# Order of roundings and low parts, pool places, subtractions and stores in a gated stage with stacked half blocks

## The chip, the cores and the metric

The kernel runs on one core of a Trainium2 chip. The metric is the device time of one execution in microseconds; the time shown for a kernel is the median of several executions. One further execution was taken with the hardware profiler, and all rows come from it. The engines are TensorE (PE; its weight loads are listed as PEld), VectorE (DVE), ScalarE (ACT), GpSimd (POOL) and SyncE (SP). SP and POOL issue nearly all DMAs; POOL does hardly anything else. Each engine executes its instructions in order.

## The reference, cut to what matters

All data are float32; S = 2048 tokens, D = 640, F = 1728.

```python
xn = _layernorm(x)
a = jnp.einsum("bsd,ed->bse", xn, dft_hid_re)
b = jnp.einsum("bsd,ed->bse", xn, dft_hid_im)
A = jnp.einsum("ts,bse->bte", dft_seq_re, a) - jnp.einsum("ts,bse->bte", dft_seq_im, b)
gate = jnp.einsum("bsd,df->bsf", xn, W_gate)
up = jnp.einsum("bsd,df->bsf", xn, W_up)
gate = gate * (gate > 0).astype(gate.dtype)
B = jnp.einsum("bsf,fd->bsd", gate * up, W_down)
return x + A + B
```

## The kernel before, in words

Every matrix product is done in split precision: an operand is rounded to a high part (a copy by ACT, the helper `copy`, L128, or the first line of `split`, L131), and the rest is its low part (a subtraction by DVE, L132 in `split`). A product is then three matmuls (`mm3`, L137 to L139: high x high, high x low, low x high), each 128x128 weights by 128x512 moving columns. Products are arranged in Strassen-Winograd fashion: seven block products with sums S1 to S4 of one operand and T1 to T4 of the other, in place of eight.

The kernel has three stages.

The first stage (`ph0`, `ph1`) normalises x and multiplies it by the sequence DFT matrices, chunk by chunk (four chunks of 512 columns). A chunk is 20 blocks, five kinds (T1, T2, B22, T3, T4) with four groups each. The function `drive` walks over the blocks of all chunks: it issues a block's loads, prepares it (subtraction L712, split L131 and L132) two positions ahead, and runs its matmuls two positions later. Beside that, `token_sets` builds the token operand of the gated stage (steps 0 to 5 for each half q of the tokens): load raw x and row statistics, `make` (subtract and scale, L394/L395 for steps 0 and 1, L417/L418 for the others), `more` (T sums, L424), `halve` (split into two parts), and a `keep` that stores them to DRAM from POOL (L401, L436, L449). `cross_sets` stacks the two parts of a half block over the 128 partitions: four loads on POOL (L464), four subtractions on DVE (L471), six stores on POOL (L475, L476). These pieces are put into the first stage by `hooks`: `at(c, name, g, f)` calls f in the preparation of that block. The hook's place is a place in the text of the program. In the first stage the order on each engine is made by a planner that works with estimated costs and readiness; only instructions that are pinned (`keep_in_program_order`, `pin`, `issue_after`) keep to the program's order. The subtractions L471 and the loads L464 are not pinned.

The gated stage (`ph2`) is a loop of 26 units, 13 column blocks of 128 for each of the two token halves, the second half of the tokens first. Here the order on PE, DVE, ACT and POOL is the written one (`manual_schedule`); SP's is still the planner's. One unit, `gate_up(n)`, has 53 matmuls. In PE's order, with the PSUM banks b1, b4, c, d: A11B11 into b1; S1T1 into b4; S2T2 onto b1; A12B21 onto c, with one short product; S3T3 onto b1; S4B22 onto b4, with one short product each onto b4 and d; A22T4 onto b1, with one short product. Each long product is six matmuls of `mm3` and one matmul with the stacked half blocks (L967); the short ones are L970. ACT copies b1 to c after the first product, b4 to d after the second, b1 to u2 after the third and b1 to u3 after the fifth, and takes the relu of c (L1003) after the fourth. PE may only write onto b1 again when the copy before has been made.

Between these, the weights of the next unit are prepared (`Weights`): SP loads the raw tile z (two units ahead); ACT rounds the half block of the fifth row (`fifth_high`, 64x512) and DVE takes its low part (`fifth_low`, L915); DVE makes the four sums (`sums`, L921 to L924); ACT rounds the sums in two parts (`high_sums(0)`, `high_sums(1)`, 128x768 each), and the own blocks and w5 (`high_own`, 128x1152 and 128x256); DVE takes the low parts of the sums (`low_sums`, 128x1024) and of the own blocks (`low_own`, 128x768), both L937. DVE also makes oa (L1017) and, in the next unit, the three `finals` (L954 to L956), after which POOL stores the result (L957, hd). Further work is put into slots of a unit by lists: `issues` (after the finals), `urgent`, `loads` (before S3T3), `besides` (after u3), `after` (after oa). It is token steps for the other half (units 1 to 9), the cross step (unit 10), loading and splitting the next token sets (`next_set`, units 11, 12 and 24), and from unit 13 on one pair of down-projection weights in each (`pair_weights`: five SP loads L1118, four DVE operations L1123 to L1126, a rounding, a low part L1132, a POOL store L1139).

`gate_up_rest` does the 64 last columns of gate and up, before the first unit for one token half and after the last for the other: relu (rg, L1062), product (hh, L1063), and a store of hh from POOL (hr, L1066). Behind the first of its two products in the second call stands `lead_split`, which prepares the first product of the last stage.

The last stage projects both results with the hidden DFT matrices and W_down (tiles rw or raws for the data, wr for raw weights, cb and wt for their splits) and stores the output.

SBUF tiles come from pools. A pool opened after another was closed takes its bytes, and a tile on bytes that an earlier tile held waits for the users of that tile. In `ph2` the left-hand pools are opened one behind the other in the order of the list; z and zs hold the weights and their sums, hob the results, cx the stacked blocks XT3, XT4 and XB22, fifth the tile w5, and sets the token work and later T sets. `late_place(i)` gives pieces of one large tile, r1, that holds other data in the first stage.

Of the kernel before, what the change touches and what calls it, by code (L numbers as in the profile page):

```python
# [7 lines left out]
F32 = mybir.dt.float32  # L8
# [4 lines left out]
P = 128  # L13
# [50 lines left out]
def fnet_reglu_kernel(  # L64
# [303 lines left out]
    def token_sets(q, step, place=None, unit=None):  # L368
# [15 lines left out]
        if step < 2:  # L384
# [56 lines left out]
            split(h.bitcast(F32R), src.bitcast(F32R), src)  # L441

        if unit:
            unit(load, made[0][0] if step > 1 else [lambda: (make(), halve("a"))], keep_whole)
            return

        def keep(name, place, view):
# [402 lines left out]
        at(c, "B22", 2 * i + 1, *([halve["mr"]] if i else halve.values()))  # L850
    load, subs, keep = cross_sets(1, work_pair)
    at(NCHUNK - 1, "T1", 0, load)
    at(NCHUNK - 1, "T1", 3, *subs[:2])
    at(NCHUNK - 1, "T2", 0, *subs[2:], lambda: defer(1, keep))

    def phase(c, names):

# [29 lines left out]


    ph2 = ExitStack()
    for n, b, side in (("prep", 2, "left"), ("tmp", 1, "left"), ("wr", 1, "left"), ("hob", 2, "left"), ("z", 2, "left"),  # L890
                       ("zs", 1, "left"), ("cx", 1, "left"), ("fifth", 2, "left"), ("sets", 1, "left"), ("gw1", 1, "right")):
        open_pools[n] = ph2.enter_context(tc.tile_pool(name=n, bufs=b, side=side, reuse_waits="tile"))
    pool = open_pools.__getitem__
    get_gw = (get_gw0, lambda: pool("gw1").tile([P, NGW], F32R, name="gw"))
# [48 lines left out]
        def low_own(self):  # L943
            self.low(self.z[:, P3 : 4 * P3], HA, 3, LOWS + 4 * 2 * P)

    issues, urgent, besides, after, loads = ({n: [] for n in range(-1, NU + 2)} for _ in range(5))
    weights, held = {}, {}
    tmp = lambda name, n=CH: pool("tmp").tile([P, n], F32, name=name)
    c0, c1 = slice(0, CH), slice(CH, W2)
# [9 lines left out]
    def gate_up(n):  # L959
        q = 1 - n // NF  # L960
        w, ahead = weights[n].w, weights.get(n + 1)

        def product(ps, a, b, x, first=False, last=False):
            for j in range(2):
                h, l = (w[:, o : o + P] for o in (a * P3 + j * P, LOWS + a * 2 * P + j * P))
                mm3(ps, (h, l), set_half(q, b, j), first and j == 0, False, not first)
            nc.tensor.matmul(ps, w[:, a * P3 + 2 * P : (a + 1) * P3], crossing[q, x], start=False, stop=last, skip_group_check=not first)  # L967
# [12 lines left out]
        if n > 0:  # L980
            finals(n - 1)
        for f in issues[n]:
            f()
        for f in urgent[n]:
            f()
        copy(c, b1)
        if ahead:
            ahead.fifth_low()
            ahead.sums()
        product(b4, S1, T1, XT1, True, True)  # L990
        copy(d, b4)
        if n == NF - 1:
            load_cross(0, "a")
        product(b1, S2, T2, XT2, last=True)
        copy(u2, b1)
        if ahead:
            ahead.high_sums(0)
        product(c, A12, B21, XB21)
        fifth_product(c, A4, 0)
        if ahead:  # L1000
            ahead.high_sums(1)
            ahead.low_sums()
        nc.scalar.activation(ob[:, c0], c, AF.Relu)  # L1003
        if n == NF - 1:
            load_cross(0, "b")
        if ahead:
            ahead.high_own()
            ahead.low_own()
        for f in loads[n]:
            f()  # L1010
        product(b1, S3, T3, XT3, last=True)
        copy(u3, b1)
        for f in besides[n]:
            f()
        product(b4, S4, B22, XB22)
# [31 lines left out]

    def gate_up_rest(q, n):
        w = rest["w"]
        rg, hh = (late_place(i) for i in (3, 4)) if n else (place(i) for i in (0, 1))  # L1050
        a, b = slice(0, REST), slice(REST, 2 * REST)
        for c in range(2):
            ps = bank()
            part = [set_half(q, (B11, B12)[c], 0), set_half(q, (B11, B12)[c], 1),
                    set_half(q, (B21, B22)[c], 0), set_half(q, (B21, B22)[c], 1), set_half(q, X4, c)]
            for k in range(KD):
                mm3(ps, (w[:, 0, k * P : (k + 1) * P], w[:, 1, k * P : (k + 1) * P]),
                    part[k], k == 0, k == KD - 1)
# [4 lines left out]
            tt(hh[a, cs], ps[a], rg[a, cs], op=OP.mult)  # L1063
            if n and c == 0:
                lead_split()
        issues[0 if n is None else NU + 1].append(lambda: nc.gpsimd.dma_start(hrest[q], hh[a]))  # L1066
# [10 lines left out]

    def token_step(step, n):

        def unit(load, make, keep):  # L1080
            issues[n - 1].append(load)
            for i, m in enumerate(make):
                besides[n + i].append(m)
            issues[n + len(make)].append(keep)

        token_sets(0, step, spot, unit)

# [19 lines left out]
    def pair_weights(k, n):  # L1107
# [26 lines left out]
        loads[n - 1].append(load)  # L1134
        besides[n].append(prepare)
        after[n].append(lows_of)
        def keep():
            z = t["z"]
            nc.gpsimd.dma_start(wparts[:, k], z[:, RA:Y21])  # L1139
            if k == NPAIR - 1:  # L1140
                h, l = (z[:REST, o + Y22 : o + Y22 + 2 * P] for o in (HIGH, LOW))
                for rows, v, o in ((0, 0, h), (0, 1, l), (REST, 0, l), (REST, 1, h)):
                    nc.gpsimd.dma_start(wend[rows : rows + REST, v * 2 * P : (v + 1) * 2 * P], o)

        issues[n + 1].append(keep)

    def pair(k0, n):

# [23 lines left out]
        lead["b"], lead["w"] = b, w  # L1172

    loads[NU - 2].append(lead_load)
    for step, n in enumerate((1, 1, 2, 4, 6, 8)):
        token_step(step, n)

    def cross_step(n):
        load, subs, keep = cross_sets(0, lambda: pool("prep").tile([P, END], F32, name="pw")[:, : 2 * W2])
        issues[n - 1].append(load)  # L1180
        besides[n] += subs
        issues[n + 1].append(keep)

    cross_step(10)
    next_set(X4, 9)
    for i, n in ((T2, 11), (T1, 11), (T3, 11)):
        next_set(i, n)
    next_set(B11, NF - 1, lambda: place(3), low=besides)
    next_set(B21, NF - 1, lambda: place(4), low=besides)
    next_set(T4, NF - 1)  # L1190
    next_set(B22, NF - 1, lambda: place(5), high=after, low=urgent, later=1)
    next_set(B12, 24, lambda: late_place(2))
# [312 lines left out]
```

## Time and profile before

| what | value |
|---|---|
| runs, median (lowest to highest) | 1043.58 us (1043.14 to 1045.24), 3 runs |
| the profiled execution | 1044.09 us |
| its span, first to last instruction | 1041.9 us |
| mean granted TensorE clock | 0.993 |
| gated stage, units 0 to 25 | about 414 to 734 us of the span |
| DMA moved | 266.43 MB, mean 256 GB/s |

How to read the rows: a wait row names the engine and the tile it works on, who released it, the total in us, the number of times and the longest. A timeline row has start, duration, engine, line, operation, out<-in, shape, count, and in brackets the idle time of that engine before it with what ended it. A row of the chain of waits has start, duration and what the time was. A stretch row has the stretch, its length, the busy time of PE, PEld, DVE, ACT and POOL with the number of instructions, the granted clock, the DMA share and GB/s. A row on DMA issues has out<-in, queue, count, KB of each and the median us from issue to landing. Times in rows count from the start of the span. PE's busy time overlaps itself a little: a matmul row lasts 0.39 us while the next one starts 0.23 us after it.

### The profile page before, as it was taken

The numbers are of one execution on the slowest core, as the hardware profiler recorded it, in microseconds if no ns is written. First come the engines' busy times: TensorE is split into PE (matmuls) and PEld (weight loads), VectorE is DVE, ScalarE is ACT, GpSimd is POOL, SyncE is SP. The second block draws the span as 40 slices with busy tenths as digits, with TensorE's granted clock in tenths as the row PEclk, the third lists the DMA queues.
The fourth block names the chain that finished last, engine by engine and source line by source line (L and its number), as shares of the span: only waits on it lengthen the run. The fifth ranks groups of instructions, "written<-read, shape, count | busy, mean of one in ns | idle before, by whom it ended". The sixth has DMA issues, their size and how long they took to land.

```text
span 1041.9 us, 12615 instructions
## 1 busy us (share of the span) xinstructions
PE 1019.1 (98%) x4498; PEld 840.7 (81%) x4498; DVE 810.7 (78%) x1085; ACT 487.2 (47%) x659; POOL 135.2 (13%) x215
## 2 busy tenths in 40 slices
PE   9999999999979999999999999999899999999998
PEld 8888888888867888778888788878688888888887
DVE  7967977999949777587778888877586896767983
ACT  5644453343432334455556665555344434443432
POOL 3521011022131001122221000101000001000000
PEclk9999999999999999999999999999899999999999
DMA  8897735859868976766659777785899477897624
GB/s 319 318 300 279 249 125 175 318 203 320 330 220 291 381 296 242 233 232 215 211 204 344 284 279 252 230 299 216 289 357 324 130 255 220 280 323 233 219 91 142
DMA packets 94142, 266.43 MB, mean 256 GB/s; under 512 B 11776, under 2 KB 32832, under 8 KB 91264
## 3 DMA queue, kind: packets, MB, share of 16 engines
q1 hardware_dynamic: 73584, 185.12, 52.1%
q0 software_dynamic: 20064, 79.97, 21.0%
q8 instruction: 35, 0.57, 0.2%
q10 hardware_dynamic: 432, 0.56, 0.1%
q14 instruction: 27, 0.22, 0.1%
HBM read 198.74 MB, written 65.81 MB: 254 GB/s over the span
## 4 chain that ended last, share of the span: by engine, by line
PE 63%; issue 24%; DMA 5%; DVE 3%; POOL 3%; ACT 1%; SPq 0%; POOLq 0%; ACTq 0%; DVEq 0%
PE ps L137 19%; PE ps L138 19%; PE ps L139 19%; PE ps L546 3%; PE ps L967 2%; DMA cx<-cross 1%; DMA wparts<-pw 1%; PE ps L970 1%; PE ps L576 1%; DMA pw<-in_wd 1%; PE ps L1350 1%; POOL set L449 1%; DMA sets_b<-rows 1%; DMA r<-in_xt 1%; ACT gw L128 0%
## 5 line engine op out<-in xcount | busy, mean ns | idle before, releaser
L131 ACT ACTIVATE cb<-rw 128x1024 fp32r<-128x1024 f32 x83 | 81.7, 987 | 138.9 <-PE ps L139 97.8
L131 ACT ACTIVATE cb<-raw 128x1024 fp32r<-128x1024 f32 x71 | 75.3, 1060 | 124.5 <-PE ps L139 116.3
L132 DVE TENSOR_TENSOR cb<-rw,cb 128x1024 fp32r<-128x1024 f32 x83 | 93.9, 1132 | 49.3 <-ACT cb L131 48.9
L132 DVE TENSOR_TENSOR cb<-raw,cb 128x1024 fp32r<-128x1024 f32 x71 | 86.8, 1222 | 37.6 <-ACT cb L131 37.2
L137 PE MATMUL ps<-cb,wt 128*128 128x512 f32 x270 | 105.9, 394 | 4.4 <-ACT wt L131 4.4
L138 PE MATMUL ps<-cb,wt 128*128 128x512 f32 x270 | 105.6, 393 | 0.0
L139 PE MATMUL ps<-cb,wt 128*128 128x512 f32 x270 | 105.4, 392 | 0.0
L138 PE MATMUL ps<-cb,xs_late 128*128 128x512 f32 x232 | 90.3, 389 | 0.0
L137 PE MATMUL ps<-cb,xs_late 128*128 128x512 f32 x232 | 90.3, 389 | 0.0
L139 PE MATMUL ps<-cb,xs_late 128*128 128x512 f32 x232 | 90.3, 389 | 0.0
L137 PE MATMUL ps<-cb,xs_early 128*128 128x512 f32 x226 | 87.9, 389 | 0.0
L138 PE MATMUL ps<-cb,xs_early 128*128 128x512 f32 x226 | 87.9, 389 | 0.0
L139 PE MATMUL ps<-cb,xs_early 128*128 128x512 f32 x226 | 87.9, 389 | 0.0
L937 DVE TENSOR_TENSOR gw<-zs,gw 128x1024 fp32r<-128x1024 f32 x26 | 31.9, 1226 | 46.4 <-ACT gw L128 46.4
L137 PEld LDWEIGHTS ps<-cb,wt 128*128 128x128 f32 x270 | 51.2, 190 | 15.5 <-ACT wt L131 4.8
L128 ACT ACTIVATE gw<-z 64x512 fp32r<-64x512 f32 (+1 forms) x52 | 46.4, 893 | 32.4 <-PE ps L967 25.9
L138 PE MATMUL ps<-xs_early,gw 128*128 128x512 f32 x156 | 60.8, 390 | 0.0
L137 PE MATMUL ps<-xs_early,gw 128*128 128x512 f32 x156 | 60.7, 389 | 0.0
L139 PE MATMUL ps<-xs_early,gw 128*128 128x512 f32 x156 | 60.7, 389 | 0.0
L138 PEld LDWEIGHTS ps<-cb,wt 128*128 128x128 f32 x270 | 51.4, 190 | 10.8
L139 PEld LDWEIGHTS ps<-cb,wt 128*128 128x128 f32 x270 | 51.1, 189 | 10.6
L131 ACT ACTIVATE cb<-tk 128x1024 fp32r<-128x1024 f32 x32 | 33.9, 1060 | 46.6 <-PE ps L139 28.9
(219 smaller groups left out, 2413.2 us busy)
## 6 DMA issues: line engine op xcount, KB each, us to landing
raw<-in_dft SPq DMA_DIRECT2D x94, 512.0 KB, 6.4
z<-in_wgu SPq DMA_DIRECT2D x26, 896.0 KB, 5.6
wd<-wparts SPq DMA_DIRECT2D x30, 512.0 KB, 5.0
wparts<-pw POOLq DMA_DIRECT2D x12, 1152.0 KB, 5.8
hd<-ob POOLq DMA_DIRECT2D x26, 512.0 KB, 3.4
rw<-hd SPq DMA_DIRECT2D x24, 512.0 KB, 7.5
tk<-in_dft SPq DMA_DIRECT2D x16, 512.0 KB, 6.8
set<-r POOLq DMA_DIRECT2D x16, 512.0 KB, 4.3
```

The lines of the kernel that those rows point to most:

```text
L128: return nc.scalar.activation(o, i, AF.Copy)
L131: nc.scalar.activation(hi, src, AF.Copy)
L132: return nc.vector.tensor_tensor(lo, src, hi.bitcast(F32), op=OP.subtract)
L137: nc.tensor.matmul(ps, wh, mh, start=first, stop=False, skip_group_check=more)
L138: nc.tensor.matmul(ps, wh, ml, start=False, stop=False, skip_group_check=more)
L139: nc.tensor.matmul(ps, wl, mh, start=False, stop=last, skip_group_check=more)
L449: nc.gpsimd.dma_start(place(v), view(part))
L546: start["pe"] = pin([nc.tensor.matmul(E[0, key], xn_part(n * SG + j, d)[v == 1], b[:, int(v == 2), j], start=False, stop=n % NH == NH - 1 ...
L576: pin([nc.tensor.matmul(E[c, key], xn_part(j, d)[v == 1], b[c][0][:, int(v == 2), j], start=j == 0 and v == 0, stop=False)])
L937: tt(self.w[:, o : o + n * 2 * P].rearrange("p (k n) -> p k n", k=n), main(src), main(self.w[:, at : at + n * P3]).bitcast(F32), op=OP.sub ...
L967: nc.tensor.matmul(ps, w[:, a * P3 + 2 * P : (a + 1) * P3], crossing[q, x], start=False, stop=last, skip_group_check=not first)
L970: nc.tensor.matmul(ps, weights[n].w5[:, a : a + P], set_half(q, X4, c)[0], start=False, stop=True, skip_group_check=True)
```

## The change

Five things are done together.

1. The order inside a unit of the gated stage. On ACT, `high_own` goes from behind the relu to behind u2; `high_sums(0)` from behind u2 to behind the relu; `high_sums(1)` from in front of the relu to behind u3. On DVE, `low_own` and `low_sums` go behind what is in `besides`, and the order of the two is exchanged. Two slots are new: `between` (after d) and `middle` (after the relu).
2. Token steps 0 and 1 of the other half: step 0 is made in unit 0, step 1 in unit 1 (both in unit 1 before), and their halves go into `between` of the next unit; the keep of step 1 goes out one unit later. The loads of both stay in front of the first unit. The high part of the next set B11 goes from `besides` to `middle`, and the low part of B21 from `besides` to `after`, in unit 12.
3. The list of pools of `ph2`: cx and fifth are opened ahead of z, zs and hob. In `gate_up_rest`, rg and hh of the second call are tiles of the pool z in place of `late_place(3)` and `late_place(4)`.
4. The hooks of the four subtractions of `cross_sets` in chunk 3: from T1 group 3 and T2 group 0 to T2 group 3 and B22 group 2; its keep is deferred from there.
5. The keeps of `pair_weights` and of `cross_step` go from `issues` of unit n + 1 to `after` of unit n.

```diff
@@ cross_sets' hooks, first stage
-    at(NCHUNK - 1, "T1", 3, *subs[:2])
-    at(NCHUNK - 1, "T2", 0, *subs[2:], lambda: defer(1, keep))
+    at(NCHUNK - 1, "T2", 3, *subs[:2])
+    at(NCHUNK - 1, "B22", 2, *subs[2:], lambda: defer(1, keep))
@@ pools of the gated stage
-    for n, b, side in (("prep", 2, "left"), ("tmp", 1, "left"), ("wr", 1, "left"), ("hob", 2, "left"), ("z", 2, "left"),
-                       ("zs", 1, "left"), ("cx", 1, "left"), ("fifth", 2, "left"), ("sets", 1, "left"), ("gw1", 1, "right")):
+    for n, b, side in (("prep", 2, "left"), ("tmp", 1, "left"), ("wr", 1, "left"), ("cx", 1, "left"), ("fifth", 2, "left"),
+                       ("z", 2, "left"), ("zs", 1, "left"), ("hob", 2, "left"), ("sets", 1, "left"), ("gw1", 1, "right")):
@@ gate_up
         copy(d, b4)
+        for f in between[n]:
+            f()
...
         copy(u2, b1)
         if ahead:
-            ahead.high_sums(0)
+            ahead.high_own()
         product(c, A12, B21, XB21)
         fifth_product(c, A4, 0)
-        if ahead:
-            ahead.high_sums(1)
-            ahead.low_sums()
         nc.scalar.activation(ob[:, c0], c, AF.Relu)
...
+        for f in middle[n]:
+            f()
         if ahead:
-            ahead.high_own()
-            ahead.low_own()
+            ahead.high_sums(0)
         for f in loads[n]:
             f()
         product(b1, S3, T3, XT3, last=True)
         copy(u3, b1)
+        if ahead:
+            ahead.high_sums(1)
         for f in besides[n]:
             f()
+        if ahead:
+            ahead.low_own()
+            ahead.low_sums()
         product(b4, S4, B22, XB22)
@@ gate_up_rest
-        rg, hh = (late_place(i) for i in (3, 4)) if n else (place(i) for i in (0, 1))
+        rg, hh = (pool("z").tile([P, NRAW], F32, name="z")[:, :W2] for _ in range(2)) if n else (place(i) for i in (0, 1))
@@ token_step
-        def unit(load, make, keep):
-            issues[n - 1].append(load)
+        def unit(load, make, halve, keep):
+            issues[max(n - 1, 0)].append(load)
             for i, m in enumerate(make):
                 besides[n + i].append(m)
-            issues[n + len(make)].append(keep)
+            if halve:
+                between[n + 1].append(halve)
+            issues[n + len(make) + bool(halve)].append(keep)
@@ pair_weights, and the same line in cross_step
-        issues[n + 1].append(keep)
+        after[n].append(keep)
@@ steps and next sets
-    for step, n in enumerate((1, 1, 2, 4, 6, 8)):
+    for step, n in enumerate((0, 1, 2, 4, 6, 8)):
...
-    next_set(B11, NF - 1, lambda: place(3), low=besides)
-    next_set(B21, NF - 1, lambda: place(4), low=besides)
+    next_set(B11, NF - 1, lambda: place(3), high=middle, low=besides)
+    next_set(B21, NF - 1, lambda: place(4))
```

More of the change, by code (lines that the diff above doesn't have):

```diff
@@ L443, in token_sets @@
         if unit:
-            unit(load, made[0][0] if step > 1 else [lambda: (make(), halve("a"))], keep_whole)
+            unit(load, made[0][0], (lambda: halve("a")) if step < 2 else None, keep_whole)
             return
@@ L944, in low_own @@
             self.low(self.z[:, P3 : 4 * P3], HA, 3, LOWS + 4 * 2 * P)
-    issues, urgent, besides, after, loads = ({n: [] for n in range(-1, NU + 2)} for _ in range(5))
+    issues, urgent, between, middle, besides, after, loads = ({n: [] for n in range(-1, NU + 2)} for _ in range(7))
     weights, held = {}, {}
@@ L1181, in cross_step @@
         besides[n] += subs
-        issues[n + 1].append(keep)
+        after[n].append(keep)
     cross_step(10)
```

## The prediction

> **What bounds the kernel now.** I read the page's busy shares first, then the waits of TensorE (PE), then stretches cut at the starts of the gated stage's units, and last the rows around each gap.
>
> ```profile
> PE 1019.1 (98%) x4498; PEld 840.7 (81%) x4498; DVE 810.7 (78%) x1085; ACT 487.2 (47%) x659; POOL 135.2 (13%) x215
> ...
> PE ps L138 <- DVE cb L132: 8.2, 1, 8.2
> PE ps L137 <- ACT wt L131: 4.4, 1, 4.4
> PE ps L137 <- ACT u L128: 3.0, 3, 1.7
> ```
>
> PE is the bound: busy 98% of the span. The matmuls stay as they are, so the change can win PE's waits and what follows them, no more. By stretches (the stretch and its length; busy time of PE, PEld, DVE, ACT, POOL; granted clock; DMA share and GB/s) the gated stage reads:
>
> ```profile
> 414.07:428.09 14.02, 12.31 (x55) 9.87 (x53) 8.72 (x13) 7.20 (x13) 0.55 (x1) 1.00 0.84 298
> 440.10:453.85 13.75, 12.63 (x55) 9.79 (x53) 11.62 (x18) 6.88 (x12) 2.74 (x5) 1.00 0.49 177
> 465.86:477.87 12.01, 12.01 (x54) 9.95 (x53) 8.81 (x14) 6.30 (x11) 2.10 (x3) 1.00 0.65 240
> 561.97:574.20 12.23, 12.23 (x54) 9.87 (x53) 10.09 (x13) 8.79 (x14) 0.54 (x1) 1.00 1.01 379
> 574.20:588.39 14.19, 12.50 (x55) 9.79 (x53) 12.80 (x20) 8.74 (x13) 0.53 (x1) 1.00 0.84 312
> 684.49:698.04 13.55, 12.63 (x54) 9.79 (x53) 11.65 (x21) 7.69 (x12) 1.07 (x2) 1.00 0.81 285
> ```
>
> An undisturbed unit takes 12.01 us for 53 matmuls. Five of 26 are longer: unit 0 by 2.01, unit 2 by 1.74, unit 12 by 0.22, unit 13 by 2.18, unit 22 by 1.54. The waits of 8.2 and 4.4 us lie outside, one in the third chunk of the first stage (it ends at 314.7), one where the gated stage ends (749.5); each is followed by slow matmuls:
>
> ```profile
> 314.70:317.90 3.20, 3.13 (x8) 2.52 (x9) 3.20 (x5) 0.00 (x0) 0.00 (x0) 0.52 0.75 260
> 749.50:754.70 5.20, 5.17 (x12) 4.11 (x13) 5.20 (x7) 4.27 (x6) 0.00 (x0) 0.50 0.59 176
> 754.70:760.00 5.30, 5.30 (x25) 4.34 (x25) 3.41 (x4) 2.84 (x4) 0.00 (x0) 1.00 0.94 315
> ```
>
> At full clock 25 matmuls start in 5.30 us (about 0.22 each), at clock 0.50 only 12 in 5.20. So the wait of 4.4 us has a tail of (23 less 12) x 0.22 = 2.5, together 6.9 us. The wait of 8.2 has one of (14 less 8) x 0.22, about 1.4: 9.6 us.
>
> The Trainium skill (TensorE: Matmul & The Clock Gate, Part 1) lets the clock drop after an idle window of about 3.4 us and rise again after about 3.4 us of work. The trace has clock 0.5 behind both long waits and behind none of the short ones, as that says; but the tail here lasts 5.2 us. By the page's 3.4 us the second wait would be worth some 0.8 us less than I take.
>
> **The change, part by part.**
>
> *Places of the pools.* cx and fifth together take as many bytes as hob (a 768 KB tile and two of 128 KB against two of 512 KB), and z and zs lie between: cx and fifth swap places with hob, z and zs stay. At the end, cx lay on the first stage's sums; now it lies on its raw tiles.
>
> ```profile
> 400.45 1.23 DVE L132 TENSOR_TENSOR cb<-raw,cb 128x1024 fp32r<-128x1024 f32 x1 [0.68 <-ACT cb L131]
> ...
> 408.65 2.97 DMA pq<-sa
> ...
> 411.75 12.07 DMA cx<-cross
> ...
> 423.87 0.50 PE ps L967
> ```
>
> The load of cx waited until the last sums were stored (408.65 + 2.97), took 12.07, and PE waited for it in unit 0. The last read of a raw tile ends at 401.7; from there even 12.07 us end at 413.8, before unit 0 starts. Unit 0's 2.01 us go. What is late next: hob, now on the sums, is first written in unit 0, which starts at 414.07, after the sums' store landed at 411.6. That cover is 2.5 us; without it the gate's copy waits, whose reader is a unit away.
>
> *rg and hh of the rest.* They move from the r1 block to two z tiles.
>
> ```profile
> 741.58 1.05 ACT L131 ACTIVATE cb<-rw 128x1024 fp32r<-128x1024 f32 x1
> 748.63 0.84 ACT L131 ACTIVATE wt<-wr 128x768 fp32r<-128x768 f32 x1 [6.00 <-issue]
> ...
> 742.70 0.53 POOL L1066 DMA_DIRECT2D hr<-r  x1 [6.76 <-DVE r L1063]
> ...
> DMA to landing us min/median/max: 5.9/5.9/5.9
> ...
> 734.73 0.38 SPq L1295 DMA_DIRECT2D wr<-in_hid  x1
> ...
> wr<-in_hid SPq DMA_DIRECT2D x1, 384.0 KB, 5.9
> rw<-hd SPq DMA_DIRECT2D x3, 512.0 KB, 9.5
> ```
>
> The first wt tile of the last stage lies on the r1 block, so its copy waits for the store of hh: 742.70 + 5.9 = 748.6, and ACT starts at 748.63. The weight itself landed at 734.73 + 5.9 = 740.6. With hh elsewhere ACT copies at 742.6 (0.84), DVE's low part is there near 745, and PE, whose wait began at 745.1 (749.5 less 4.4), goes on. The z tiles are free (unit 25 is the last), and what lies on them in the last stage is its B21 input, due two products later. Bounds: all 6.9 us, or none if the next wait takes its place (rival 2); the rows show nothing else that holds the copy, so I take 6.9.
>
> *Order within a unit.* Shown in unit 13, the worst:
>
> ```profile
> 582.33 1.72 ACT L128 ACTIVATE gw<-zs 128x768 fp32r<-128x768 f32 x2 [2.34 <-DVE zs L922]
> 583.96 0.58 ACT L1003 ACTIVATE ob<-ps 128x512 f32<-128x512 f32 x1
> 584.44 1.15 ACT L128 ACTIVATE gw<-z 128x1152 fp32r<-128x1152 f32 x1
> 585.49 0.40 ACT L128 ACTIVATE w<-z 128x256 fp32r<-128x256 f32 x1
> 585.80 0.58 ACT L128 ACTIVATE u<-ps 128x512 f32<-128x512 f32 x1
> ...
> 580.37 0.69 DVE L915 TENSOR_TENSOR z<-z,gw 64x512 f32<-64x512 f32 x1
> 581.68 0.56 DVE L922 TENSOR_TENSOR zs<-zs,z 128x384 f32<-128x384 f32 x1
> 584.09 1.23 DVE L937 TENSOR_TENSOR gw<-zs,gw 128x1024 fp32r<-128x1024 f32 x1 [0.91 <-ACT gw L128]
> 585.62 0.96 DVE L937 TENSOR_TENSOR gw<-z,gw 128x768 fp32r<-128x768 f32 x1 [0.31 <-ACT gw L128]
> 586.50 0.42 DVE L1123 TENSOR_TENSOR pw<-pw 128x256 f32<-128x256 f32 x1
> ```
>
> PE cannot overwrite b1 until u3 is copied (585.80); in ACT's queue that copy stands behind five others, the first of which waits for DVE's sums. After the change ACT takes own + w5 (1.15 + 0.40), which need only L915: 581.1 to 582.7; the gate 0.58 (583.2); one sum rounding 0.85 (584.1); u3 0.58 (584.7). PE wants it after 45 of the unit's matmuls, near 584.5, so I leave 0.3 of 2.18. Unit 12 has one more copy on that path (the high part of B11, now in `middle`, about 1 us): I put it at 0.3. Unit 2 was long because the halves of both token steps sat in unit 1 and pushed DVE and ACT into unit 2 (DVE 11.62 us there). Now one step is made in unit 0 and one in unit 1, and each half falls into ACT's idle time behind d. Its 1.74 go. Units 2, 12 and 13: 4.14 less 0.6, so 3.5.
>
> The other side: both low parts now come last on DVE, behind `besides`. From the unit's start DVE has three finals of about 0.7, L915 0.69 and four sums of 0.56 (5.0 us), a pair's four operations of 0.42 (6.7), then the own low of 0.96 (behind own, about 8). The sums' low waits for the second sum rounding, which follows u3: its product ends after 36 matmuls (8.3), so 8.9 + 0.85, and the low part ends at 11, in unit 13 near 12.7. PE wants them at its 3rd and 10th matmul, 12.5 and 14.0. This is a cover of 1.3 us at worst and 3 as a rule, so I cost it at nothing; with the cover gone it is rival 4.
>
> *The two stores.* Pair stores (and the cross stores) go out behind the low parts, no longer behind the next unit's finals: Pool issues them some 3 us earlier, ahead of hd, which is ready later anyway.
>
> ```profile
> wparts<-pw POOLq DMA_DIRECT2D x12, 1152.0 KB, 5.8
> ...
> 664.25 11.22 DMA wparts<-pw
> ...
> 684.96 0.44 DVE pw L1123
> ```
>
> Unit 22 was long because one store took 11.22 us, twice the median; the load into its tile followed it, and DVE started that pair only at 684.96, when unit 22 (684.49) had begun. 3 us earlier puts it at 682, before the end of its own unit. Bounds 0 and 1.54; I take 1.5.
>
> The Trainium skill (DMA: Bandwidth & Descriptors, Queues, rings and completion order) has each DMA engine take turns between the queues that have work, so an earlier store only takes its time from the loads beside it; by that rule unit 22 keeps its 1.5 us. The trace has stores of half and of twice that length under the same kinds of transfer and settles nothing.
>
> *The subtractions.* Rows of DVE and POOL around the 8.2 us, and one of DVE's later:
>
> ```profile
> 312.89 0.69 DVE L471 TENSOR_TENSOR r<-r 128x512 fp32r<-128x512 f32 x1 [12.50 <-DMA r<-set]
> ...
> 307.84 0.55 POOL L464 DMA_DIRECT2D r<-set  x1
> ...
> 341.13 2.36 DVE L712 TENSOR_TENSOR tk<-tk,raw 128x1024 f32<-128x1024 f32 x2
> ```
>
> DVE stood for 12.50 us at the first subtraction, whose fourth load was issued only at 307.84; the low part that PE needed (cb L132) stood behind it. But the program places that subtraction behind chunk 3's fourth T1 block, whose own subtraction is the second of the two at 341.13. It ran 29 us ahead of its place: the planner takes it as a filler as soon as it believes the loads landed, and nothing pins it. The new place is six blocks further back, unpinned as well. What pulled it forward over ten blocks should pull it over sixteen. Bounds 0 and 9.6; I take 0, since the row shows that the place did not bind.
>
> **Sum.** 2.0 + 6.9 + 3.5 + 1.5 = 13.9 us. The profiled execution took 1044.09 us (its span of 1041.9 and 2.2 around it), 0.5 above the runs' median of 1043.58. So 1030.2 profiled, 1029.7 for the median.
>
> **Rivals.**
> 1. The later place does free DVE, and the wait that ends at 314.7 goes too. For it: in its new place the operands would have landed long before. Against: the 29 us. 1029.7 less 9.6 is 1020.1.
> 2. The boundary keeps its gap: another load takes the place of hh's store, and rw loads took 9.5 us there. Against: what the first product needs landed at 740.6. 1029.7 + 6.9 = 1036.6.
> 3. Units 12, 13 and 22 keep most of their loss, DVE being late in them for its own load (12.80 and 11.65 us busy). 1029.7 + 3 = 1032.7.
> 4. Slower: the low parts come too late for the next unit, since a pair's operations wait for a load and the low parts now stand behind them. It decides once they end over 3 us later than I reckon in most of the 25 units. At 1 us past that in each: 1029.7 + 25 = 1054.7; break-even is 0.56 us. Against it: DVE idles 2 to 3 us in a unit (8.81 to 10.09 of 12.01 busy), and the earlier store brings the loads forward.
>
> **How the numbers follow.** Forecast 0.46, rival 1 0.30, rival 3 0.10, rival 2 0.08, rival 4 0.06. The range runs from rival 1 with 2.6 us of slack to beyond rival 3: 1017.5 to 1034. This kernel's measurement tells about 0.2% (2 us) from no change. All cases but the last are faster by more; 0.03 I keep for losses that cancel: faster 0.92, same 0.03, slower 0.05.
>
> **What would show it.** cx loaded before 414 and unit 0 at 12.0 us; ACT's first wt copy near 742.6 less what was won before, and no clock of 0.5 there; all units at 12.0 but for 0.3 in 12 and 13; the wparts store near 12.5 us into its unit. L471 idle for some 12 us in front of a low part of the third chunk bears out the planner's argument; its absence, with a time near 1020, is rival 1. PE waiting for DVE's gw (L937) at unit starts would prove me wrong.

## The result and the profile after

The changed kernel took 1030.14 us (median of 4 runs, 1029.97 to 1032.61) beside 1043.42 us for the kernel before: a ratio of 0.9875, 95% interval 0.9856 to 0.9893. The forecast was 1029.7 us. The profiled execution took 1029.97 us, its span is 1027.9 us.

The page's busy shares after the change:

```profile
PE 1014.6 (99%) x4498; PEld 840.0 (82%) x4498; DVE 808.8 (79%) x1085; ACT 488.1 (47%) x659; POOL 135.3 (13%) x215
```

and the waits of TensorE (us in total, times, longest):

```profile
PE ps L138 <- DVE cb L132: 9.0, 1, 9.0
PE ps L119 <- PEq L1506: 0.8, 1, 0.8
PE ps L576 <- DVE xs_early L337: 0.2, 1, 0.2
```

Of the profile before, the row of unit 0's wait belongs beside them:

```profile
PE ps L967 <- DMA cx<-cross: 1.7, 1, 1.7
```

One long wait is left: for DVE's low part in the first stage, 9.0 us where it was 8.2. The waits for `wt` (4.4), `u` (3.0) and `cx` (1.7) are gone. Stretches of the profile after (columns as in the prediction): units 0, 2, 12, 13 and 22, and then 6 us on either side of 740 us, where the last stage has begun:

```profile
414.84:426.85 12.01, 12.01 (x54) 9.95 (x53) 8.06 (x12) 7.04 (x12) 0.55 (x1) 1.00 0.79 275
438.87:450.88 12.01, 12.01 (x55) 9.95 (x53) 10.61 (x17) 6.94 (x12) 1.68 (x3) 1.00 0.42 151
559.00:571.01 12.01, 12.01 (x54) 9.95 (x53) 11.01 (x15) 9.29 (x14) 0.53 (x1) 1.00 1.01 392
571.01:583.03 12.02, 12.02 (x55) 9.95 (x54) 11.85 (x19) 8.29 (x14) 0.53 (x1) 1.00 0.80 284
...
679.13:691.15 12.02, 12.02 (x55) 9.95 (x54) 9.72 (x17) 7.16 (x12) 1.07 (x2) 1.00 0.79 287
733.99:740.00 6.01, 6.01 (x28) 5.00 (x27) 5.39 (x8) 5.35 (x8) 1.08 (x2) 1.00 1.05 406
740.00:746.00 6.00, 6.00 (x29) 4.95 (x27) 5.19 (x7) 4.40 (x6) 0.00 (x0) 1.00 1.06 407
```

All five units are at 12.01 or 12.02 us with TensorE busy from end to end, and so are the other 21; the start of the last stage runs at clock 1.00.

TensorE runs the same 4498 matmuls in the same order in all the kernels of this study, so the time between the same two matmuls can be subtracted from one profile to the next. The table gives this for stretches between fixed matmuls (named by what lies there; us against the profile before; minus is shorter). The last column is the end of the last matmul.

| kernel | start, to 30 us | wait in chunk 3 | chunk 4 | unit 0 | unit 2 | units 12, 13 | 14 to 22 | 23 to the rest | boundary | sum |
|---|---|---|---|---|---|---|---|---|---|---|
| the change | -0.10 | +0.93 | -0.06 | -2.01 | -1.73 | -2.39 | -1.53 | 0 | -7.10 | -13.99 |
| a_subs_back | +0.99 | +1.50 | -0.06 | -2.01 | -1.73 | -2.39 | -1.53 | 0 | -7.10 | -12.34 |
| a_pin | +0.04 | -9.88 | +9.27 | -2.01 | -1.73 | -2.39 | -1.53 | 0 | -7.10 | -15.32 |
| a_pin_mid | +0.11 | -9.88 | +8.23 | -2.01 | -1.73 | -2.39 | -1.53 | 0 | -7.10 | -16.31 |
| a_pin_back | +1.13 | -9.88 | -0.06 | -2.01 | -1.73 | -2.39 | -1.53 | 0 | -7.10 | -23.58 |
| a_stores_back | -0.16 | +0.01 | -0.06 | -2.01 | -1.73 | -1.73 | -1.53 | 0 | -7.10 | -14.29 |
| a_lows_late | +0.58 | +0.93 | -0.06 | -2.01 | -1.73 | +6.50 | +1.95 | +1.94 | -7.10 | +1.00 |
| b_rest_z | -0.02 | +0.95 | -0.06 | -0.15 | -0.01 | +0.01 | +0.52 | 0 | -7.10 | -5.86 |
| b_pools | -0.01 | -0.48 | -0.06 | -2.01 | -0.01 | +0.04 | -1.27 | 0 | +0.30 | -3.49 |
| b_order | -0.05 | -0.17 | +0.05 | -1.34 | +0.51 | -0.63 | -1.53 | 0 | -0.23 | -3.39 |
| b_order_sets | +0.49 | +1.41 | -0.06 | -1.08 | +2.10 | -2.39 | -1.53 | 0 | -0.01 | -1.06 |
| b_tokens | -0.04 | +0.20 | -0.06 | -1.10 | -1.73 | 0 | +0.02 | 0 | +0.24 | -2.45 |
| b_stores | +0.90 | +0.53 | -0.06 | -0.87 | -0.01 | 0 | -1.53 | 0 | -0.34 | -1.36 |

A name with `a_` is the changed kernel with something altered, with `b_` the kernel before with one part of the change (b_order_sets has two). The table is read by columns. Where a transfer decides, a stretch that no edit touches still varies from profile to profile: over a range of 1.3 us in unit 0 and at the start, 2.0 in chunk 3, 1.8 in units 14 to 22 and 0.6 at the boundary. In chunk 4 and units 2, 12 and 13 it is the same to 0.1 us.

The runs were taken in several groups, in which the kernel before had medians of 1042.1 to 1043.4 us; a ratio below is to the kernel before in the same group, so times of two groups compare only to about 1 us. Medians and ratios leave out slow runs, of the kernels here one of b_stores (1719.59 us). Of b_pools, b_order, b_order_sets, b_tokens and b_stores the interval reaches 1.0: their times alone show no gain, and what is said of them is read from one profile each.

### The profile page after: what moved, and what is told of

The parts are those of the page before. It is cut to its first block, busy times and chain, and to the rows that moved or that the text cites. A ratio compares the mean times of both kernels' runs of the same rounds, so it can differ in the third digit from the quotient of the medians.

```text
span 1027.9 us, 12621 instructions
## 1 busy us (share of the span) xinstructions
PE 1014.6 (99%) x4498; PEld 840.0 (82%) x4498; DVE 808.8 (79%) x1085; ACT 488.1 (47%) x659; POOL 135.3 (13%) x215
## 4 chain that ended last, share of the span: by engine, by line
PE 93%; issue 4%; POOL 1%; DVE 1%; DMA 1%; ACT 0%; POOLq 0%; DVEq 0%; ACTq 0%
PE ps L138 27%; PE ps L139 27%; PE ps L137 27%; PE ps L967 4%; PE ps L546 3%; PE ps L970 2%; PE ps L576 1%; PE ps L1358 1%; POOL set L449 1%; DMA cross<-r 0%; PE ps L1363 0%; DVE cb L132 0%; DMA r<-in_x 0%; POOL r L464 0%; POOL pq L685 0%
## 5 line engine op out<-in xcount | busy, mean ns | idle before, releaser
L128 ACT ACTIVATE ps<-ps 128x512 f32<-128x512 f32 (+1 forms) x53 | 30.6, 578 | 59.8 <-PE ps L967 55.4
```

Source lines behind the costliest of these rows:

```text
L128: return nc.scalar.activation(o, i, AF.Copy)
```

## The experiments

### The subtractions: their place, and whether it binds

The changed kernel with the old places (a_subs_back):

```diff
-    at(NCHUNK - 1, "T2", 3, *subs[:2])
-    at(NCHUNK - 1, "B22", 2, *subs[2:], lambda: defer(1, keep))
+    at(NCHUNK - 1, "T1", 3, *subs[:2])
+    at(NCHUNK - 1, "T2", 0, *subs[2:], lambda: defer(1, keep))
```

> The changed kernel with only the subtractions of the first stage's cross operands put back to their two old places (behind the fourth T1 block and the first T2 block of the fourth chunk), free as before. Theory: the place does not bind, DVE takes them in the third chunk in both cases; 1030.1 us within 1 us, with the same wait near 315 us. Rival: the later place made the wait longer or shorter by itself (the wait was 8.2 us before and is 9.0 after): a difference of 0.8 us, 1029.3 us, and no more. Second rival: the old place hurts the fourth chunk: over 1032 us.

The changed kernel with the subtractions kept in program order (a_pin):

```diff
-            return lambda: nc.vector.tensor_tensor(o().bitcast(F32R), i0(), i1(), op=OP.subtract)
+            def run():
+                i = nc.vector.tensor_tensor(o().bitcast(F32R), i0(), i1(), op=OP.subtract)
+                return tc.keep_in_program_order(i) if q else i
+            return run
```

> The changed kernel with one difference: the four subtractions of the first stage's cross operands (L471) are kept at their program place, in the fourth chunk, and may no longer run ahead. Theory: the wait of 9.0 us that is left (TensorE behind DVE's low part in the third chunk, at 315.5 us) comes only from these subtractions running ahead of their loads; with its tail at clock 0.50 it costs 9.2 + 0.4 + 1.4 = 11.0 us, so the time is 1030.1 - 11.0 = 1019.1 us (1018.5 to 1020.5), and the subtractions run after 340 us with no idle time of DVE in front of them. Rival A: the load itself (its issue on POOL at 308 us) holds something else up, and a wait of several us turns up in another place: 1024 to 1030 us. Rival B: the pin makes DVE wait in the fourth chunk instead: 1030 us or more.

Both edits together (a_pin_back):

> The changed kernel with the four subtractions at their old places (behind the fourth T1 block and the first T2 block of the fourth chunk) and kept in program order there. Theory: the pin is what counts and the place does nothing, since the loads have landed (at about 313 us) long before the old place (about 341 us): 1019.1 us, as with the pin at the new places. Rival: the old place is too early even when it is kept (the low parts of T1 and T2 blocks are then late by the 0.6 us of each subtraction): up to 4 x 0.6 = 2.4 us more than with the pin at the new places.

Measured (median, and in brackets the ratio to the kernel before with its 95% interval): a_subs_back 1029.99 us (0.9888, 0.9872 to 0.9903), a_pin 1028.33 us (0.9869, 0.9853 to 0.9884), a_pin_back 1019.18 us (0.9781, 0.9763 to 0.9798), the fastest of all. DVE's rows of the changed kernel around the wait (start, length, what; the idle time before it in brackets):

```profile
313.63 0.69 DVE L471 TENSOR_TENSOR r<-r 128x512 fp32r<-128x512 f32 x1 [13.34 <-DMA r<-set]
314.24 1.22 DVE L132 TENSOR_TENSOR cb<-raw,cb 128x1024 fp32r<-128x1024 f32 x1
```

and POOL's:

```profile
308.45 0.55 POOL L464 DMA_DIRECT2D r<-set  x1
```

With the late places the subtraction still stands in chunk 3, as early as before; DVE stood 13.34 us at it until its last load, issued at 308.45, had landed. So the place did not bind, in either direction: in a_subs_back too the four subtractions run from 313.9 us on, and its time is within 0.2 us of the change (its profile is 1.65 us longer, at the start and in chunk 3, where profiles vary anyway). The wait in chunk 3 is decided by where that subtraction floats: with the pin 9.88 us go in every one of the three kernels (8.56 from one matmul to the next less the usual 0.22, and the tail).

But a_pin won only 1.8 us over the change by the medians, 1.3 by the profiles, where the theory had 11. Its longest wait of TensorE:

```profile
PE ps L137 <- ACT cb L131: 6.6, 1, 6.6
```

The longest wait for a DMA in SP's queue from 340 to 400 us (the next is 3.6 us):

```profile
SPq L792 <- DMA cross<-r: 7.2, 1, 7.2
```

And two steps of the chain of waits there, which end in TensorE's wait:

```profile
376.71 14.03 DMA raw<-in_dft
390.76 1.23 DVE raw L715
```

The late place was harmless only because it was ignored. Once it binds, the third store of the results (L479 there) leaves at 366.14 and lands at 374.37. The next loads of the operand sets (L792) go onto the same block and wait for that landing in SP's queue for 7.2 us; then three loads of 1024 KB and one more go out in one go, and the input loads behind them take 14.03 us (landed at 390.74; in a_pin_back they took 8.0 at the median). With the old place, pinned, those three loads were out at 348.5. In size this is rival A, but the cause is neither rival's: it is the late store of the results, not the load of the operands. a_pin_back came to within 0.1 us of its theory's time, but the theory's words that the place does nothing were wrong: with the pin the two places are 9.2 us apart.

The pin, with the last two one block earlier, behind T2 group 3 (five loads stand between the two blocks; the expectation counts two blocks) (a_pin_mid):

```diff
-    at(NCHUNK - 1, "T2", 3, *subs[:2])
-    at(NCHUNK - 1, "B22", 2, *subs[2:], lambda: defer(1, keep))
+    at(NCHUNK - 1, "T2", 3, *subs, lambda: defer(1, keep))
```

> The changed kernel with the subtractions of the first stage's cross operands kept in program order, the last two brought forward by two blocks (all four behind the fourth T2 block of the fourth chunk). With the pin at the change's own places the third store of the results left at 366.1 us and landed at 374.4; SP's queue stood there for 7.2 us, since the next loads go onto the same block, and four input loads behind it came late; TensorE waited 6.6 us. Theory: the wait follows that landing one for one; the third store leaves near 364 us, lands 2 us (368 to 372) earlier or more, and the wait shrinks by as much: 1022 to 1026 us. Rival: the wait has another cause (the 14 us that the input loads took) and stays near 6.6 us: 1028 us.

Measured: 1027.61 us (0.9847, 0.9819 to 0.9876; 2 runs). TensorE's longest wait in a_pin_mid:

```profile
PE ps L137 <- ACT cb L131: 4.9, 1, 4.9
```

The store landed 2.78 us earlier (371.59), the wait shrank by 1.64, the stretch by 1.04. Not one for one: the input loads left 3.08 us earlier and landed only 1.58 us earlier, behind the large loads issued ahead of them, which landed 3.1 to 3.7 us after one another. The theory's 1022 to 1026 us missed. The landing of the store decides when the queue goes on; how long the backlog then takes is the other part, which this run does not split further.

### The parts of the change alone

rg and hh alone (b_rest_z):

```diff
-        rg, hh = (late_place(i) for i in (3, 4)) if n else (place(i) for i in (0, 1))
+        rg, hh = (pool("z").tile([P, NRAW], F32, name="z")[:, :W2] for _ in range(2)) if n else (place(i) for i in (0, 1))
```

> The kernel before with one part of the change: rg and hh of the rest at the gated stage's end lie in two z tiles, not on the r1 block. Theory: ACT's copy of the first weight tile of the last stage no longer waits for the store of hh; the wait of 4.4 us at the boundary and its tail of 2.5 us at clock 0.50 both go: 1043.4 - 6.9 = 1036.5 us, and no stretch of clock 0.50 near 750 us. Rival A (the wait goes, the clock's drop has another cause): 1043.4 - 4.4 = 1039.0 us. Rival B (another wait takes its place, such as the 9.5 us loads of rw): 1041 to 1043.4 us. By the Trainium skill (TensorE: Matmul & The Clock Gate, Part 1), whose 3.4 us of work bring the clock back, the tail would be worth 1.7 us and the time 1037.3 us.

Measured: 1036.94 us (0.9951, 0.9935 to 0.9966). The boundary is 7.10 us shorter, the same as in the whole change; no wait for `wt` is left. Of the prediction's 6.9 this confirms both halves: 4.56 us go at the first matmul behind the wait and about 2.5 in the ones after it, so the tail was not shorter than the sum took it. The other columns moved by +1.2 together (chunk 3 +0.95); the loss of unit 22 turned up in unit 21 here, 2.06 us long.

The pools alone (b_pools):

```diff
-    ... ("wr", 1, "left"), ("hob", 2, "left"), ("z", 2, "left"), ("zs", 1, "left"), ("cx", 1, "left"), ("fifth", 2, "left"), ...
+    ... ("wr", 1, "left"), ("cx", 1, "left"), ("fifth", 2, "left"), ("z", 2, "left"), ("zs", 1, "left"), ("hob", 2, "left"), ...
```

> The kernel before with only the places of the pools changed (cx and fifth swap with hob). Theory: the load of cx starts once the last raw tile is read (near 402 us) and not after the last store of the sums (411.6 us); unit 0 falls from 14.02 to 12.0 us: 1043.4 - 2.0 = 1041.4 us. Rival: hob on the sums' place makes the gate's copy wait for that store instead, and some of the 2.0 us stays.

Measured: 1042.43 us (0.9994, 0.9979 to 1.0009). In the profile unit 0 is 2.01 us shorter and no wait for cx is left; nothing else comes in its place there. In the changed kernel's profile the load leaves at 402.5 and takes 4.5 us:

```profile
L823 SPq DMA_DIRECT2D cx<-cross x1: 326/326/326, 402.5 to 402.5; - x1
...
DMA to landing us min/median/max: 4.5/4.5/4.5
```

The table's column for unit 0 also shows that before's 2.01 was the longest of its kind: the kernels that keep the old places lost 0.7 to 1.9 there (2.01 less 1.34 to 0.15). In four of them (b_order, b_tokens, b_stores, b_order_sets) the same load took 10.7 to 11.2 us; in the profile before 12.07.

The order in the unit alone (b_order; here and below the lines `if ahead:` are left out):

```diff
-            ahead.high_sums(0)
+            ahead.high_own()
         product(c, A12, B21, XB21)
...
-            ahead.high_sums(1)
-            ahead.low_sums()
         nc.scalar.activation(ob[:, c0], c, AF.Relu)
...
-            ahead.high_own()
-            ahead.low_own()
+            ahead.high_sums(0)
...
         copy(u3, b1)
+            ahead.high_sums(1)
         for f in besides[n]:
             f()
+            ahead.low_own()
+            ahead.low_sums()
```

> The kernel before with only the order inside a unit changed: own rounding ahead of the sums' two, the sums' second rounding behind the copy of u3, both low parts last; token steps, the high part of B11 and the stores stay. Theory: unit 13 falls from 14.19 to 12.0 us (the copy of u3 no longer stands behind the sums' roundings), unit 12 keeps 0 to 0.2, unit 2 keeps its 1.7 (its cause is the two token steps' halves), unit 22 keeps its 1.5 (its cause is the late load): about 1043.4 - 2.2 = 1041.2 us. Rival A: the order also cures units 2 and 22, since in every late unit the copy of u3 stood behind the sums: 1043.4 - 5.4 = 1038.0 us. Rival B: the low parts, last now, come too late in the units whose own DVE work is longest (2, 13, 22): one of them grows.

Measured: 1041.54 us (0.9994, 0.9979 to 1.0009), and in the profile, beside a shorter unit 13, a new wait of TensorE:

```profile
PE ps L139 <- DVE gw L937: 3.3, 2, 1.9
```

Unit 12 is at 12.01 and unit 13's old wait is gone, but units 2 and 13 now begin with one: TensorE waited 1.9 us until 441.15 and 1.3 until 574.92 for their low parts, so unit 2 grew to 14.26 and unit 13 only fell to 13.77. That is rival B, and the mechanism of the prediction's fourth rival. DVE's rows before the second wait:

```profile
571.63 2.36 DVE L1106 TENSOR_TENSOR xs_early<-pw,xs_early 128x1024 fp32r<-128x1024 f32 x2 [2.96 <-ACT xs_early L128]
573.91 0.95 DVE L937 TENSOR_TENSOR gw<-z,gw 128x768 fp32r<-128x768 f32 x1
```

The low parts stood behind an input's low part of 2.36 us that waited 2.96 us for its high part. Unit 22 became whole, though the stores' code was not touched: ten of the twelve pair stores now leave 15.5 us after their unit's start; before they left after 15.8 to 18.6.

The same, with the places of two inputs (b_order_sets; `middle` is run behind the gate's function):

```diff
-    next_set(B11, NF - 1, lambda: place(3), low=besides)
-    next_set(B21, NF - 1, lambda: place(4), low=besides)
+    next_set(B11, NF - 1, lambda: place(3), high=middle, low=besides)
+    next_set(B21, NF - 1, lambda: place(4))
```

> The kernel before with the order inside a unit, and the places of two inputs of the last units of the first half (the high part of B11 behind the gate's function, the low part of B21 behind the unit's last sum); token steps, pools, rest and stores stay. With the order alone units 2 and 12 or 13 grew, TensorE waiting for DVE's low parts (gw, L937) by 1.9 and 1.3 us. Theory: these two inputs' parts held up the low parts near 573 us; that wait goes and units 12 and 13 are at 12.0 us together, while unit 2 stays at 14.3, its low parts behind a token step's operations. Rival: the wait near 573 us stays, and it is the token steps or the pair's load that the low parts stand behind.

Measured: 1042.12 us (0.9989, 0.9978 to 1.0001). With the two inputs out of the way units 12 and 13 are 2.39 us shorter together, both at 12.01, as in the change. Unit 2 has its wait of 1.9 us for the low parts again, and 1.6 more by a tail at clock 0.57 (below): theory on both counts, but for the tail.

The token steps alone (b_tokens, shortened; `between` is run behind the copy of d, `halve` splits steps 0 and 1 into their two parts):

```diff
-            issues[n - 1].append(load)
+            issues[max(n - 1, 0)].append(load)
...
+            if halve:
+                between[n + 1].append(halve)
-            issues[n + len(make)].append(keep)
+            issues[n + len(make) + bool(halve)].append(keep)
...
-    for step, n in enumerate((1, 1, 2, 4, 6, 8)):
+    for step, n in enumerate((0, 1, 2, 4, 6, 8)):
```

> The kernel before with only the token steps moved: the first is made in unit 0 and the second in unit 1, and the halves of each fall behind the copy of d in the unit after. Theory: unit 2 falls from 13.75 to 12.0 us, nothing else changes: 1043.4 - 1.7 = 1041.7 us. Rival: the halves (DVE's 1.2 us and ACT's 1.1 us) move the loss into unit 1 or keep it in unit 2, as the sums' roundings still stand before the copy of u3: 1043 to 1044 us.

Measured: 1041.79 us (0.9987, 0.9975 to 1.0). Unit 2 is 1.73 us shorter, no unit beside it grew. So unit 2 is the token steps', and it is the token steps' move that lets the new order stand in unit 2: the order without it makes unit 2 longer (b_order, b_order_sets).

The stores alone (b_stores; the same line in the pairs and in the cross operands):

```diff
-        issues[n + 1].append(keep)
+        after[n].append(keep)
```

> The kernel before with only the two kinds of stores moved (the pair's and the cross operands' store go out behind the low parts, not behind the next unit's finals). Theory: the pair stores are issued some 3 us earlier in a unit, the loads into their tiles follow, and the loss of 1.5 us in unit 22 goes: 1043.4 - 1.5 = 1041.9 us. Rival (by the Trainium skill, DMA: Bandwidth & Descriptors, Queues, rings and completion order, an earlier store only takes turns with the loads beside it): unit 22, or the unit ahead of it, keeps about 1.5 to 2 us: 1043.4 us. A store that still takes over 8 us, with the load behind it landing over 10 us into its unit, would bear the rival out.

Measured: 1042.68 us (0.9994, 0.997 to 1.0018). In the profile unit 22 is whole, all pair stores but two took 4.4 to 5.4 us, and the pairs' loads, all but the last, landed before their unit began. In b_stores and in the changed kernel alike, by the page's DMA issues (KB each, median us to landing):

```profile
wparts<-pw POOLq DMA_DIRECT2D x12, 1152.0 KB, 4.4
hd<-ob POOLq DMA_DIRECT2D x26, 512.0 KB, 3.8
```

An earlier store did not take its time from the loads here: its own median fell from 5.8 to 4.4 us, and that of the loads of z from 5.6 to 4.7 in b_stores; only the stores of hd became longer, from 3.4 to 3.8. The Trainium skill (DMA: Bandwidth & Descriptors, Queues, rings and completion order) has each DMA engine take turns between queues with work; by that, the prediction said, unit 22 would keep its 1.5 us, and the run did not bear that out. Why the stores became shorter no run here shows.

### Two tests of the changed kernel

The stores put back (a_stores_back; the same line in the pairs and in the cross operands):

```diff
-        after[n].append(keep)
+        issues[n + 1].append(keep)
```

> The changed kernel with only the two kinds of stores put back behind the next unit's finals. The prediction's step: unit 22 or one beside it gets its 1.5 us again, 1030.1 + 1.5 = 1031.6 us. Theory after the runs of single parts (the order alone and the stores alone each made unit 22 whole): the order already issues the pair's store earlier (15.5 us after the unit's start, against 15.8 to 18.6), so no unit grows and the time stays at 1030.1 us; the stores' move is then worth nothing beside the order. The pair's store goes out near 15.5 us in its unit and its load lands 2 to 4 us into the next but one, not before its start.

Measured: 1030.58 us (0.9876, 0.9847 to 0.9904; 2 runs). Units 14 to 22 stay whole, unit 13 is 0.66 us longer (12.68). So beside the order the stores are worth 0.7 us at most, not in unit 22: there either of the two edits is enough.

The low parts one step later (a_lows_late):

```diff
-            ahead.low_own()
-            ahead.low_sums()
         product(b4, S4, B22, XB22)
         fifth_product(b4, A4, 1)
         tt(oa, b4, u2, op=OP.add)
         for f in after[n]:
             f()
+            ahead.low_own()
+            ahead.low_sums()
```

> The changed kernel with both low parts of the next unit's weights moved one step further back, behind the sum of oa and the pair's low part. It measures the cover that the prediction gave the low parts (1.3 us at worst, about 3 as a rule; beyond it each us late in 25 units is 25 us). In a unit with a pair: oa ends about 10.9 us into the unit, the pair's low part 11.9, the own low part 12.8, the sums' 14.0; TensorE wants them at 12.5 and 14.0. Theory: 0.3 us late in the 12 units with a pair, none in the others: 1030.1 + 4 = 1034 us (1031 to 1038), and TensorE waits for DVE's gw (L937). Rival A: the cover is larger than reckoned: no change, 1030.1 us. Rival B: lateness runs up from unit to unit, as the finals and the sums behind them come later too: over 1045 us.

Measured: 1043.99 us (1.0007, 0.9982 to 1.0032; the runs from 1040.62 to 1049.49), 13.9 us over the change and outside both the theory and its rivals. Its waits of TensorE:

```profile
PE ps L138 <- DVE cb L132: 7.7, 1, 7.7
PE ps L139 <- DVE gw L937: 5.9, 3, 2.6
```

Units 14 to 24 are 12.40 or 12.41 us each, so the low parts are late by the 0.3 to 0.4 us expected in each. Units 12, 13 and 25, which follow the units where token sets are prepared too (`next_set`), lost 4.5, 4.0 and 1.5 us; those the expectation had left out. One step further back on DVE would have eaten the whole gain of the change.

## Why the prediction was right

Term by term, with the profile's stretches (forecast, measured):

- Pools, 2.0: 2.01. Both halves of the argument showed: the load no longer waits for the sums' store, and unit 0 shows no wait of TensorE. The term was sized from one draw of the transfer, though; the draws of other kernels were 0.7 to 1.9, so that it fits to 0.01 is luck.
- Boundary, 6.9: 7.10. ACT copies the first weight tile at 735.63; the forecast was 742.6 less what was won until then, 6.9, so 735.7. ACT's rows after:

```profile
734.68 1.05 ACT L131 ACTIVATE cb<-rw 128x1024 fp32r<-128x1024 f32 x1
735.63 0.84 ACT L131 ACTIVATE wt<-wr 128x768 fp32r<-128x768 f32 x1
```

- Order, 3.5: 4.12 (1.73 and 2.39). The step that failed is the 0.6 left in units 12 and 13. For unit 13 it let the copy of u3 end at 584.7, 10.5 us into the unit; in the changed kernel it ends after 9.7 us (unit 13 starts at 571.01, unit 14 at 583.03). ACT's rows after:

```profile
577.48 1.17 ACT L128 ACTIVATE gw<-z 128x1152 fp32r<-128x1152 f32 x1 [0.86 <-DVE z L915]
...
580.07 0.59 ACT L128 ACTIVATE u<-ps 128x512 f32<-128x512 f32 x1
```

and DVE's:

```profile
576.76 0.69 DVE L915 TENSOR_TENSOR z<-z,gw 64x512 f32<-64x512 f32 x1
...
581.83 1.22 DVE L937 TENSOR_TENSOR gw<-zs,gw 128x1024 fp32r<-128x1024 f32 x1
...
592.75 1.23 DVE L937 TENSOR_TENSOR gw<-zs,gw 128x1024 fp32r<-128x1024 f32 x1 [1.13 <-ACT gw L128]
```

Two things were taken wrongly: L915 stands 5.75 us into the unit and not at its old 6.17, and the four copies from own to u3 take 2.59 us from start to start where the sum of their rows gave 2.98 (each row's length reaches into the next row): 0.4 us each, together the 0.8. The low part of the sums ends 12.04 us into unit 13 and 10.95 into unit 14: the prediction had 12.7 and 11. Its cost of nothing was right, and its cover as thin as said (a_lows_late). What the prediction did not say is that this cover exists only with the token steps and the two inputs moved as well (b_order).
- Stores, 1.5 in unit 22: 1.53, but not theirs alone. The order gives the same. The kernels with neither lost 0.3 (b_pools), 1.5 (before, b_tokens) and 2.1 us (b_rest_z, in unit 21), so this size was a draw too. Right sum, wrong share. The prediction's remark that the trace has stores of half that length is wrong: the twelve took 5.03 to 11.22 us, the median being 5.8.
- Subtractions, 0: the place did not bind, as argued from the 29 us. The wait even grew by 0.93 us in the stretch (a draw: 7.3 to 9.0 us over the kernels that have it).

The errors (+0.2 boundary, +0.6 order, -0.9 wait) cancel to 0.1: the mechanisms were right, but that the sum is so close is luck. Rival 1's price of 9.6 was right too (9.88), but its condition was not met; a pin meets it, and then the change's own place costs 9.3 us again. Rivals 2 and 3 did not come about. Rival 4 did not either, but its mechanism showed twice (b_order, a_lows_late), and in size as it was reckoned: 0.39 us more in each of eleven units for low parts 0.3 to 0.4 us late.

## What to carry to other kernels

A line's place in the program proves nothing where a scheduler may move it: compare the time at which it ran with its place first, and if it floats, pin it before you tune the place. Then look for what the place would do once it binds: here a late store cost TensorE 6.6 us, 20 us later. Parts of a change that look separate may be each other's cover, so measure a part alone only together with the question what it leaned on; and a wait read from one profile that ends with a transfer is one draw, here 0.7 to 2.0 us.

## What had not been expected of the hardware

The clock drops after shorter waits than the prediction took. Two stretches each, in turn of b_order_sets, b_order and a_lows_late (for the first two a wait at the start of unit 2 and the stretch behind it, for the third the stretches behind its first two waits; the clock is the third number from the right):

```profile
441.20:443.40 2.20, 0.28 (x2) 0.00 (x0) 1.59 (x3) 1.20 (x2) 0.00 (x0) 1.00 0.00 0
443.40:447.40 4.00, 3.98 (x10) 3.14 (x11) 3.93 (x6) 0.58 (x1) 0.06 (x1) 0.57 0.64 224
```

```profile
438.90:441.10 2.20, 0.30 (x2) 0.00 (x0) 1.57 (x3) 1.22 (x2) 0.00 (x0) 1.00 0.00 0
441.10:445.10 4.00, 3.95 (x17) 3.30 (x18) 3.94 (x6) 1.16 (x2) 0.04 (x1) 1.00 0.67 228
```

```profile
562.90:566.50 3.60, 3.58 (x9) 2.81 (x10) 3.53 (x5) 0.58 (x1) 0.16 (x1) 0.54 1.03 401
...
578.90:582.00 3.10, 3.08 (x10) 2.49 (x11) 3.06 (x5) 0.58 (x1) 0.00 (x0) 0.72 1.02 415
```

Nearly the same wait (1.94 and 1.95 us) at the same place was followed by clock 0.57 in the one kernel and by 1.00 in the other; the waits of 2.63 and 2.08 us of a_lows_late were followed by 0.54 and 0.72. Behind waits of 1.2 to 1.7 us the clock did not drop in any of eight cases in these profiles. Behind the waits that brought it down 7 to 14 matmuls were slow (most of them about 0.43 us from start to start, against 0.22), so a tail cost 1.5 to 3.0 us here; it does not grow with the wait (1.6 us behind 9.0, 3.0 behind 4.0). The Trainium skill (TensorE: Matmul & The Clock Gate, Part 1) names an idle window of about 3.4 us that runs free of the kernel: that the drop depends on the phase of this window agrees with these rows, that a whole window must be idle does not, since the longest of these three waits was 2.63 us.
